# Products that nothing reads, ahead of and in the first part of an attention and two-layer kernel

## The chip, the cores and the metric

The kernel runs on one core of a Trainium2 chip. The metric is the device time of one execution in microseconds (us); less is better. A core has the matrix engine TensorE (PE; PEld is its loading of weights), VectorE (DVE), ScalarE (ACT), GpSimd (POOL) and SyncE (SP), which here only starts transfers (DMA). Each engine works through its own list of instructions in order and waits where an input is not there.

## The reference

Three stages follow one another. `_attn_ref` is a linear attention with decay, `_moe_ref` and `_moe2_ref` are products with weights:

```python
for t in range(S):                        # S = 768; B, H = 4, 8; D = 48
    state = alpha[:, :, t, :, None] * state + np.einsum('bhd,bhe->bhde', k[:, :, t], v[:, :, t])
    y[:, :, t] = np.einsum('bhd,bhde->bhe', q[:, :, t], state)
...
a = x @ w1                                # x: 3072 x 384, w1, w2: 384 x 1024
b = x @ w2
h = a * b @ w3                            # 1024 x 1024
return h @ w_out                          # 1024 x 384
...
h = x @ w_in                              # 384 x 2048
g = h * np.clip(h + 3.0, 0.0, 6.0) / 6.0
return g @ w_out                          # 2048 x 384
```

All inputs are float32 or, the weights, 64 bit floats.

## The kernel before, in words

**Attention** is cut into 24 units: six blocks of 512 tokens times four pairs of heads. A unit passes through steps `a0` to `a9` (`b5` to `b13` from unit 8 on). `a0` transposes the decay on PE into aT (four transposes, L301) and scans it on DVE (L313 to L324) into the running product P and its reverse r. `a1` transposes q (qT) and scales it (Q). `a2` uses the tile KT as scratch for a check on ACT (L341, L342) and transposes k (kT). `a3` multiplies kT by r into KT (DVE L347), so KT waits for L342. `a5` transposes KT back (kb, L385), and ACT copies that to Kn (L388). `score` makes the products sc of Q and KT (L358, plain fp32) and masks them into A; `a6` makes the state products u (L398) and the states T; `a8` the outputs py (L438, L446), which ACT copies to ys (L451). `a9` splits the result for the next stage.

**Weights** arrive as 64 bit words (`raw`, three buffers). A piece takes three ACT instructions (L72, L73, L76) and two on DVE (L81, L85) and then usually a split into a high and a low part (ACT L148, POOL L149). `w3` and `w_out` are folded into one matrix: `fold_t` transposes a piece of w3 (w3ps, L663) and splits it, `fold_mm` multiplies (facc; `mm3`, L152 to L154, three products for each pair). `l1_a` and `l1_b` are the products with w1 and w2 (w, the same lines), `l2` those with the folded matrix (acc, L723 to L726), `l3` and `l4` the second layer.

**Order.** A prologue runs over 33 gaps, `for g in range(npro)` at L872: each gap does the attention steps that are due (`attn_gap(g)`), some pieces of weight (`ws.step`) and, in a few gaps, a fold. A unit begins every sixth gap. The main loop (L883) then does an L1 step with three gaps each, so that attention runs on beside it. The written order is not the order of the engines: a scheduler goes through the program with a model of the times and puts each engine's instructions in an order of its own; only from step 46 of the main loop on is the written order kept (`MANUAL_FROM`). `ps_acc` has one PSUM buffer each of the tags acc0, acc1 and acc2; the folds use acc0 and acc1, the L2 sums all three. The tag asb in `tmp` has one buffer, which `l1_a` writes.

Of the kernel before, what the change touches and what calls it, by code (L numbers as in the profile page):

```python
# [8 lines left out]
F32 = mybir.dt.float32  # L9
# [9 lines left out]
P = 128  # L19
# [4 lines left out]
TB = 512  # L24
# [34 lines left out]
TBF = 1  # L59
ED = 16  # L60
SG = (5, 7, 9, 11, 14)
MANUAL_FROM = 46
RAWS = 3
RAW2 = 3
# [27 lines left out]
def attn_moe_kernel(  # L92
# [16 lines left out]
    nc = tc.nc  # L109
# [3 lines left out]
    def pool(stack, name, bufs, **kw):  # L113
        return stack.enter_context(tc.tile_pool(name=name, bufs=bufs, **kw))
# [6 lines left out]
    tmp = pool(main, "tmp", 2)  # L121
# [7 lines left out]
    ps_acc = pool(main, "ps_acc", 1, space=PSUM)  # L129
# [13 lines left out]
    over = const.tile([P, NB * NP], F32, tag="over", name="over")  # L143
    ones = const.tile([P, 2], F32, tag="ones", name="ones")
    nc.vector.memset(ones, 1.0)

    def split(hi, lo, x):
        nc.scalar.copy(out=hi, in_=x)  # L148
        nc.gpsimd.tensor_tensor(out=lo, in0=x, in1=hi.bitcast(F32), op=ALU.subtract)  # L149
# [462 lines left out]

    stages = {0: a0, 1: a1, 2: a2, 3: a3, SG[0]: a5, SG[1]: score, SG[2]: a6, SG[3]: a8, SG[4]: a9}
    stages2 = {0: a0, 1: a1, 2: a2, 3: a3, 5: b5, 6: b6, 9: b9, 12: b12, 13: b13, 15: a9}
# [3 lines left out]
    def begin(i):  # L618
        return 6 * i - min(max(i - U1, 0) // 2, 3)

    def attn_gap(g):
        for i in range(g // 6 - 2, g // 6 + 2):
            kk = g - begin(i)
            todo = stages if i < U1 else stages2 if begin(i) - begin(i - 1) == 6 else stages3
            if 0 <= i < len(units) and kk in todo:
                todo[kk](i)
# [32 lines left out]
    def fold_t(f, half):  # L659
        ps = ps_mm.tile([P, 4, P], F32, tag="mm", name="w3ps")  # L660
        w = w3n.pop((f, half))
        for g in range(4):
            nc.tensor.transpose(ps[:, g, :], w[:, g * P:(g + 1) * P], ident)  # L663
        hi = fs.tile([P, 4, P], F32R, tag="w3hi", name="w3hi")
        lo = fs.tile([P, 4, P], F32R, tag="w3lo", name="w3lo")
        nc.scalar.copy(out=hi, in_=ps)
        full = cv.tile([P, 4, P], F32, tag="u", name="w3full")
        nc.scalar.copy(out=full, in_=ps)
        nc.gpsimd.tensor_tensor(out=lo, in0=full, in1=hi.bitcast(F32), op=ALU.subtract)
        w3t[f, half] = (hi, lo)  # L670

    def fold_mm(f):
        if f < FOLDACC:
            acc = ps_acc.tile([P, DM], F32, tag=f"acc{f % KD}", name="facc")
        else:
            acc = ps_at.tile([P, DM], F32, tag="at", name="facc")
        for g in range(NM1):
            hi, lo = w3t[f, g // 4]
            mm3(acc, hi[:, g % 4, :], lo[:, g % 4, :], wo[g][0], wo[g][1], g == 0, g == NM1 - 1)
        hi = wts.tile([P, DM], F32R, tag=f"w34hi{f}", name="w34hi")  # L680
        lo = wts.tile([P, DM], F32R, tag=f"w34lo{f}", name="w34lo")
        nc.scalar.copy(out=hi, in_=acc)
        nc.vector.tensor_tensor(out=lo, in0=acc, in1=hi.bitcast(F32), op=ALU.subtract)
        w34[f] = (hi, lo)
# [110 lines left out]
    acc2 = {}  # L795
# [63 lines left out]
    for m in range(1, NM1 + 1):  # L859
        new = w3_items(m + AHEAD) + col_items(m)  # L860
        rest += new
        n = len(new)
# [5 lines left out]
    for what in INIT.split():  # L868
        n = int(what[1:])
        {"a": load_aqk, "v": load_v, "w": ws.issue}[what[0]](n)  # L870
    npro = 3 * LEAD
    for g in range(npro):  # L872
        attn_gap(g)
        ws.step(PC.get(g, 0))
        for f in PT.get(g, ()):
            fold_t(f, 0)
            fold_t(f, 1)
        if g in PF:
            fold_mm(PF[g])
# [3 lines left out]
    for si in range(n1 + 1):  # L883
        if si == MANUAL_FROM:
            manual.enter_context(tc.manual_schedule())
        g = npro + 3 * si
# [300 lines left out]
```

## Time and profile before

| | us |
|---|---|
| median of 3 runs | 910.4 (905.47 to 912.03) |
| profiled execution | 908.21 |
| its span, first to last instruction | 906.3 |
| PE busy | 870.2 (96%) |
| PEld, DVE, ACT, POOL busy | 735.0, 487.7, 380.6, 338.9 |

Times in the trace are us from the start of the span. A busy PE need not be one at its peak: matmuls are pipelined, so that in dense stretches the distance of two starts is shorter than the duration shown. A plain fp32 product gives two records in the trace, a transpose or a product of split (fp32r) operands one. "idle before <-X" is the engine's wait just before, and what ended it. The granted clock is the share of full speed (2.4 GHz) that TensorE was given; half is 1.2 GHz.

### The profile page before, as it was taken

What the parts mean: (1) busy time and instruction counts of PE and PEld (TensorE: products, weight loads), DVE (VectorE), ACT (ScalarE), POOL (GpSimd) and SP (SyncE); (2) the same over time, 40 slices, a digit from 0 to 9 for tenths busy, and PEclk for the clock granted to TensorE, in tenths of its full rate; (3) what the DMA queues carried; (4) which work ended last, traced back from release to release, by engine and by line L of the source; (5) the groups of instructions that cost most, each with busy time, mean ns of one, the idle gap of its engine ahead of it and who ended that gap; (6) DMA issues with size and microseconds to landing.
All of it is one profiled execution on the core that took longest, in us unless ns stands there. A gap on an engine that the chain in (4) does not pass through costs nothing.

```text
span 906.3 us, 16328 instructions
## 1 busy us (share of the span) xinstructions
PE 870.2 (96%) x6202; PEld 735.0 (81%) x6202; DVE 487.7 (54%) x844; ACT 380.6 (42%) x781; POOL 338.9 (37%) x310
## 2 busy tenths in 40 slices
PE   6889999999999999999899999999999999999995
PEld 5668888877787777777778898898898898888984
DVE  5987686767676778742646564333333333333331
ACT  5888888533343333434866663122121121121111
POOL 1544454412212222222755574342342342342331
PEclk9979999999999999999999999999999999999998
DMA  8785655453444544202543331001002002001001
GB/s 202 189 200 152 190 133 155 65 101 58 68 86 70 85 87 64 71 10 86 163 135 118 104 111 59 1 12 59 1 12 59 1 12 59 1 12 36 0 1 39
DMA packets 183431, 69.45 MB, mean 77 GB/s; under 512 B 154289, under 2 KB 172849, under 8 KB 183345
## 3 DMA queue, kind: packets, MB, share of 16 engines
q1 hardware_dynamic: 178992, 65.18, 30.5%
q10 hardware_dynamic: 4352, 3.15, 1.2%
q8 instruction: 51, 0.84, 0.4%
q14 instruction: 36, 0.29, 0.1%
HBM read 54.13 MB, written 9.44 MB: 70 GB/s over the span
## 4 chain that ended last, share of the span: by engine, by line
PE 80%; DMA 7%; ACT 5%; DVE 4%; SPq 2%; issue 2%; ACTq 0%; DVEq 0%
PE acc L808 7%; PE acc L811 7%; PE acc L809 7%; PE h L154 7%; PE h L153 7%; PE h L152 7%; PE w L152 6%; PE w L153 6%; PE w L154 6%; PE acc L726 3%; PE acc L723 3%; PE acc L724 3%; DMA raw<-in_moe_w_in 2%; DMA raw<-in_moe_w 2%; DMA out<-ot 1%
## 5 line engine op out<-in xcount | busy, mean ns | idle before, releaser
L149 POOL TENSOR_TENSOR glo<-g,ghi 128x512 fp32r<-128x512 f32 x96 | 126.0, 1313 | 236.8 <-ACT ghi L148 236.8
L785 DVE TENSOR_SCALAR t<-h 128x512 f32<-128x512 f32 x96 | 66.3, 691 | 236.3 <-PE h L154 236.3
L148 ACT CAST ghi<-g 128x512 fp32r<-128x512 f32 x96 | 59.7, 622 | 289.1 <-DVE g L787 267.3
L808 PE MATMUL acc<-wo2hi,ghi 128*128 128x384 f32 x384 | 130.7, 340 | 2.9 <-ACT ot L822 2.8
L809 PE MATMUL acc<-wo2lo,ghi 128*128 128x384 f32 x384 | 128.7, 335 | 0.0
L152 PE MATMUL w<-xhi,w 128*128 128x512 f32 x288 | 115.5, 402 | 7.3 <-ACT asb L703 7.3
L149 POOL TENSOR_TENSOR ablo<-ab,abhi 128x512 fp32r<-128x512 f32 x48 | 66.1, 1378 | 129.0 <-ACT abhi L148 121.9
L154 PE MATMUL h<-yhi,wilo 128*128 128x512 f32 x288 | 113.8, 395 | 0.0
L154 PE MATMUL w<-xhi,w 128*128 128x512 f32 x288 | 113.6, 394 | 0.0
L153 PE MATMUL h<-ylo,wihi 128*128 128x512 f32 x288 | 113.5, 394 | 0.0
L152 PE MATMUL h<-yhi,wihi 128*128 128x512 f32 x288 | 113.5, 394 | 0.0
L153 PE MATMUL w<-xlo,w 128*128 128x512 f32 x288 | 113.5, 394 | 0.0
L811 PE MATMUL acc<-wo2hi,glo 128*128 128x384 f32 x384 | 82.4, 335 | 0.0
L808 PEld LDWEIGHTS acc<-wo2hi,ghi 128*128 128x128 f32 x384 | 71.9, 187 | 9.6 <-ACT ot L822 4.4
L809 PEld LDWEIGHTS acc<-wo2lo,ghi 128*128 128x128 f32 x384 | 72.1, 188 | 4.3
L787 DVE SCALAR_TENSOR_TENSOR g<-t,h 128x512 f32<-128x512 f32 x96 | 66.0, 688 | 11.5 <-POOL glo L149 1.0
L152 PEld LDWEIGHTS w<-xhi,w 128*128 128x128 f32 x288 | 54.0, 188 | 20.8 <-ACT asb L703 9.7
L81 DVE SCALAR_TENSOR_TENSOR w<-u,w 128x384 uint32<-128x384 uint32 (+1 forms) x72 | 50.4, 702 | 37.4 <-ACT w L76 36.0
L811 PEld LDWEIGHTS acc<-wo2hi,glo 128*128 128x128 f32 x384 | 68.0, 188 | 0.0
L154 PEld LDWEIGHTS h<-yhi,wilo 128*128 128x128 f32 x288 | 53.9, 187 | 13.2
L154 PEld LDWEIGHTS w<-xhi,w 128*128 128x128 f32 x288 | 54.1, 188 | 11.7
L153 PEld LDWEIGHTS w<-xlo,w 128*128 128x128 f32 x288 | 54.1, 188 | 11.0 <-POOL xlo L149 0.4
(131 smaller groups left out, 1544.2 us busy)
## 6 DMA issues: line engine op xcount, KB each, us to landing
raw<-in_moe_w_out SPq DMA_DIRECT2D x24, 384.0 KB, 3.4
raw<-in_moe_w SPq DMA_DIRECT2D x16, 512.0 KB, 4.7
raw<-in_moe_w SPq DMA_DIRECT2D x16, 384.0 KB, 3.1
raw<-in_moe_w_in SPq DMA_DIRECT2D x16, 384.0 KB, 3.8
y<-yt SPq DMA_DIRECT2D x18, 256.0 KB, 2.3
yraw<-y SPq DMA_DIRECT2D x18, 256.0 KB, 2.9
vn<-in_v SPq DMA_DIRECT2D x32, 96.0 KB, 2.5
out<-ot SPq DMA_DIRECT2D x32, 96.0 KB, 2.2
```

Of the source, the lines that this page charges most:

```text
L81: nc.vector.scalar_tensor_tensor(out=low, in0=u.bitcast(U32), scalar=3, in1=low, op0=ALU.logical_shift_left, op1=ALU.bitwise_or,)
L148: nc.scalar.copy(out=hi, in_=x)
L149: nc.gpsimd.tensor_tensor(out=lo, in0=x, in1=hi.bitcast(F32), op=ALU.subtract)
L152: nc.tensor.matmul(out=dst, lhsT=lh, rhs=rh, start=start, stop=False)
L153: nc.tensor.matmul(out=dst, lhsT=lh, rhs=rl, start=False, stop=False)
L154: nc.tensor.matmul(out=dst, lhsT=ll, rhs=rh, start=False, stop=stop)
L723: nc.tensor.matmul(out=acc1[o], lhsT=wh[:, sl], rhs=hi, start=m == 0, stop=False)
L785: nc.vector.tensor_scalar(out=t, in0=ps, scalar1=3.0, scalar2=0.0, op0=ALU.add, op1=ALU.max)
L787: nc.vector.scalar_tensor_tensor(out=g, in0=t, scalar=6.0, in1=ps, op0=ALU.min, op1=ALU.mult)
L808: nc.tensor.matmul(out=acc2[o], lhsT=hi[:, sl], rhs=wh, start=m == 0, stop=False)
L809: nc.tensor.matmul(out=acc2[o], lhsT=hi[:, sl], rhs=wl, start=False, stop=False)
L811: nc.tensor.matmul(out=acc2[o], lhsT=lo[:, o * P:(o + 1) * P], rhs=wh, start=False, stop=m == NM2 - 1)
```

## The change

A tile `hot` of 128x512 is set to 0.5 by DVE, and `run_hot(n)` issues n products of its 128 first columns with its 256 first, in plain fp32, into the PSUM tile `heat`, which nobody reads. Five are written ahead of everything, and one behind the attention steps of each of the gaps 1 to 23: 28 in all. `heat` takes the tag acc2, `hot` the tag asb.

```diff
+HEAT = range(1, 24)
...
+    heat = ps_acc.tile([P, TB], F32, tag="acc2", name="heat")
+    hot = tmp.tile([P, TB], F32, tag="asb", name="hot", bufs=1)
+    nc.vector.memset(hot, 0.5)
+
+    def run_hot(n):
+        for _ in range(n):
+            nc.tensor.matmul(out=heat[:, :2 * P], lhsT=hot[:, :P], rhs=hot[:, :2 * P], start=True, stop=True)
+
+    run_hot(5)
...
     for g in range(npro):
         attn_gap(g)
+        if g in HEAT:
+            run_hot(1)
         ws.step(PC.get(g, 0))
```

The scheduler gives the engines another order with it. Lines of the changed kernel stand 11 further down (13 in the loops at the end), so its L312 is L301 of before.

PE at the start of the program, before:

```order
L301 MATMUL aT<-cs,al 112x128 x4
L301 MATMUL qT<-cs,qn 112x128 x4
L301 MATMUL kT<-cs,kn 112x128 x4
L385 MATMUL kb<-cs,KT 128x112 x4
L301 MATMUL aT<-cs,al 112x128 x4
L358 MATMUL sc<-Q,KT 128x128 x8
L663 MATMUL w3ps<-cs,w 128x128 x4
```

And PE there with the change:

```order
L154 MATMUL heat<-hot 128x256 x12
L312 MATMUL aT<-cs,al 112x128 x4
L312 MATMUL qT<-cs,qn 112x128 x4
L312 MATMUL kT<-cs,kn 112x128 x4
L154 MATMUL heat<-hot 128x256 x7
L674 MATMUL w3ps<-cs,w 128x128 x4
L154 MATMUL heat<-hot 128x256 x8
L396 MATMUL kb<-cs,KT 128x112 x4
L312 MATMUL aT<-cs,al 112x128 x4
L369 MATMUL sc<-Q,KT 128x128 x2
L674 MATMUL w3ps<-cs,w 128x128 x4
L369 MATMUL sc<-Q,KT 128x128 x2
```

The 28 products stand in four places, 12, 7, 8 and (behind the last row shown) 1, all of them ahead of unit 1's scores; the first w3ps has moved ahead of kb.

DVE at the start, before (edge is the scan's second operand, w a piece of weight):

```order
L145 MEMSET ones 128x2
L611 MEMSET edge 128x513
L313 TENSOR_SCALAR edge<-aT 112x4
L316 MEMSET aT 112x4
L317 SCALAR_TENSOR_TENSOR P<-aT,edge 112x512
```

And with the change:

```order
L146 MEMSET ones 128x2
L150 MEMSET hot 128x512
L622 MEMSET edge 128x513
L82 SCALAR_TENSOR_TENSOR w<-u,w 128x512
L86 SCALAR_TENSOR_TENSOR w<-raw,w 128x512
L324 TENSOR_SCALAR edge<-aT 112x4
L327 MEMSET aT 112x4
L328 SCALAR_TENSOR_TENSOR P<-aT,edge 112x512
```

The first piece of weight has moved from behind unit 0's KT to ahead of unit 0's first instruction.

ACT from the second piece of weight to L342 of unit 1, before, all of it:

```order
L72 ACTIVATE u<-raw 128x512
L73 ACTIVATE w<-raw,seven 128x512
L365 COPY A<-sc 128x512
L341 ACTIVATE KT<-al,amid 128x448
L76 ACTIVATE w<-w,seven 128x512
L666 CAST w3hi<-w3ps 128x512
L72 ACTIVATE u<-raw 128x384
L73 ACTIVATE w<-raw,seven 128x384
L342 ACTIVATE KT,over<-KT,adev 128x448
```

And the last twelve rows of the same stretch with the change, ahead of which stand thirteen more from the second piece on:

```order
L677 CAST w3hi<-w3ps 128x512
L679 COPY w3full<-w3ps 128x512
L334 COPY r<-edge 112x1
L73 ACTIVATE u<-raw 128x384
L74 ACTIVATE w<-raw,seven 128x384
L376 COPY A<-sc 128x512
L352 ACTIVATE KT<-al,amid 128x448
L159 CAST wohi<-w 128x384
L77 ACTIVATE w<-w,seven 128x384
L73 ACTIVATE u<-raw 128x384
L74 ACTIVATE w<-raw,seven 128x384
L353 ACTIVATE KT,over<-KT,adev 128x448
```

Where eight instructions stood ahead of L342 there are 24 now, most of them for pieces of weight that came later before.

## Rows read from the trace of the kernel before

**Rows 1.** The page, part 2: granted clock in 40 slices, in tenths.
```profile
PEclk9979999999999999999999999999999999999998
```

**Rows 2.** Busy time of each engine by stage; the first line names the columns.
```profile
core 0: us, PE busy (x) PEld busy (x) DVE busy (x) ACT busy (x) POOL busy (x), PEclk, DMA share, GB/s
0.00:20.00 20.00, 12.86 (x74) 10.62 (x76) 11.15 (x22) 9.52 (x18) 2.77 (x20) 1.00 0.87 204
...
47.00:68.00 21.00, 18.10 (x110) 14.70 (x111) 17.43 (x29) 17.43 (x38) 9.81 (x10) 0.68 0.80 202
68.00:280.00 212.00, 210.24 (x1900) 169.58 (x1900) 152.84 (x282) 123.94 (x266) 78.60 (x79) 1.00 0.51 110
```

**Rows 3.** Order of time, PE, 0 to 32: start, us, engine, line, operation, shapes, records.
```profile
4.45 1.07 PE L301 MATMUL aT<-cs,al 128*112 128x128 f32 x4 [4.45 <-DMA al<-in_alpha]
...
10.20 1.01 PE L385 MATMUL kb<-cs,KT 112*128 112x112 f32 x4 [2.64 <-DVE KT L347]
...
11.99 3.09 PE L358 MATMUL sc<-Q,KT 48*128 48x128 f32 x16
...
18.77 2.16 PE L438 MATMUL py<-A,vn 128*64 128x128 f32 x16
...
20.85 0.66 PE L663 MATMUL w3ps<-cs,w 128*128 128x128 f32 x4
...
23.40 0.62 PE L301 MATMUL aT<-cs,al 128*112 128x128 f32 x4 [0.90 <-ACT w3hi L666]
...
24.74 1.16 PE L358 MATMUL sc<-Q,KT 48*128 48x128 f32 x8
...
31.21 1.09 PE L438 MATMUL py<-A,vn 128*64 128x128 f32 x16
```

**Rows 4.** Order of time, PE, 64 to 85.
```profile
64.35 1.03 PE L446 MATMUL py<-Q,T 48*48 48x128 f32 x12 [0.52 <-DVE T L420]
...
68.34 0.34 PE L154 MATMUL facc<-wohi,w3lo 128*128 128x384 f32 x1
...
81.89 0.60 PE L301 MATMUL aT<-cs,al 128*112 128x128 f32 x4
...
84.18 0.33 PE L154 MATMUL facc<-wohi,w3lo 128*128 128x384 f32 x1
...
84.36 0.33 PE L152 MATMUL facc<-wohi,w3hi 128*128 128x384 f32 x1
```

**Rows 5.** Order of time, DVE, 0 to 22.
```profile
0.96 0.49 DVE L611 MEMSET edge<- 128x513 f32 x1
...
5.64 0.17 DVE L313 TENSOR_SCALAR edge<-aT 112x4 f32<-112x4 f32 x1 [4.20 <-PE aT L301]
...
9.46 0.69 DVE L347 TENSOR_TENSOR KT<-kT,r 112x512 f32<-112x512 f32 x1
...
12.21 0.69 DVE L85 SCALAR_TENSOR_TENSOR w<-raw,w 128x512 uint32<-128x512 uint32 x1
...
21.15 0.69 DVE L347 TENSOR_TENSOR KT<-kT,r 112x512 f32<-112x512 f32 x1 [0.70 <-ACT KT L342]
```

**Rows 6.** Order of time, ACT, second raw piece, L342 of units 1, 3, 5.
```profile
16.03 0.68 ACT L72 ACTIVATE u<-raw 128x512 f32<-128x512 f32 x1 [1.04 <-DMA raw<-in_moe_w]
...
20.38 0.66 ACT L342 ACTIVATE KT<-KT,adev 128x448 f32<-128x448 f32 x1
...
41.12 0.65 ACT L342 ACTIVATE KT<-KT,adev 128x448 f32<-128x448 f32 x1
...
75.71 0.67 ACT L342 ACTIVATE KT<-KT,adev 128x448 f32<-128x448 f32 x1
```

**Rows 7.** The chain that ended last: start, us, what.
```profile
72.19 1.09 PE sc L358 x8
...
98.11 0.23 PE w L152
```

## Prediction

> **What bounds the kernel now.** I read the clock line of the page first, then the busy times by stage, then PE, DVE and ACT in order of time, then the chain. The clock line [rows 1] is full nearly everywhere and dips in the third of its forty slices. By stage [rows 2], PE is busy 210.24 of 212 us from 68 to 280: from there on the time is PE's own list of work. Before 68 us PE waits for others: it has 12.86 busy us in the first 20, and 18.10 of 21 from 47 to 68 at a granted clock of 0.68. So only the first 80 us can change, and one mark tells by how much: the transposes of attention unit 6 (aT) start at 81.89 [rows 4]. In the order of before and of the change PE has the same products ahead of that mark (except the 28 new ones) and nearly the same order behind it, and DVE and ACT have converted 18 pieces of weight by then in both. If PE stays busy behind it, the time moves as that mark moves.
>
> The early low clock does not stand in the granted figure (1.00 for the first 20 us), but in durations [rows 3]: four transposes take 1.07 us at 4.45 and 0.62 at 23.40, the four of kb 1.01 at 10.20; the sixteen sc records 3.09 against 2 x 1.16; the sixteen py 2.16 against 1.09. The rise stands between the py at 18.77 and the w3ps at 20.85 (0.66). Eight groups of transposes at about 0.4 over, 0.77 for sc and 1.07 for py make 5.0 us of slow work. The dip from 47 to 68 costs 21 x (1 - 0.68) = 6.7 us of PE, in a stretch in which PE also had idle time. Together 11.7 us is all that a better clock could return.
>
> The Trainium skill (TensorE: Matmul & The Clock Gate, Part 1) puts the cost of warming up under 1% of a typical span, which would be 9 us here and speaks against a large gain. The early 5.0 us (0.6%) agrees, while with the later dip the rows come to 1.3%.
>
> **The change, part by part.** *The products.* Not five at the beginning and one per gap: in the order 12 stand ahead of everything, 7 behind the first twelve transposes (aT, qT, kT of unit 0), 8 ahead of kb and 1 in unit 0's scores. All 28 lie before unit 1's work, so nothing new runs near 47 us. A product of 128x256 in plain fp32 does not occur before. Bounds: from below, a py product of 128 columns, 1.09/8 = 0.14 us; from above, twice an sc product, 2 x 1.09/4 = 0.55 us [rows 3, 7]. I take 0.55, since sc is a plain fp32 product run one after another as these are. 28 x 0.55 = 15.4 us at full clock (3.9 by the lower bound). At the low clock sc shows up to twice this, so 1.1 us. The Trainium skill (FP8 and Floating Point Precision, TensorE Precision Notes) counts four passes for true fp32; with 0.23 us for a one-pass product of 512 columns [rows 7] that is an estimate of 0.46 each and 12.9 us in all.
>
> *When they end.* The memset of hot on DVE is as long as the one of edge, 0.49 us [rows 5], and ends near 1.5 us; PE starts there instead of at 4.45. How soon the clock rises has two rows: 10 us after work became dense at 10.20 [rows 3], and 4.0 us after 64.35, where records are back at 0.34 at 68.34 [rows 4]. In the quick case 4 us bring 3.6 products, and the other 8.4 take 4.6: the twelve end at 10.1. In the slow case 10 us bring 9.1 and the rest takes 1.6: 13.1. aT then follows 6 to 9 us later than before.
>
> *What hides that.* DVE's list has turned too: the first weight piece (L81, L85) now stands ahead of aT's scan. Its raw data and ACT's three steps are not sooner, so it ends where it did, at 12.21 + 0.69 = 12.90 [rows 5], and only then does the chain of unit 0 start, at 12.90 instead of 5.64: 7.3 us later when aT is there at 10.7, and 0.8 more in the slow case. The four and a half us from 5.64 to KT's end (9.46 + 0.69) follow: KT at 17.4. PE then still has qT, kT and w3ps (1.9 us) and 7 + 8 products (8.2): kb starts at 21 instead of 10.20, or at 23.5. ACT reads kb as its 13th instruction after 16.03, at about 22.5 by the pace below, which covers the quick case and leaves 1.6 us of the slow one open.
>
> *Unit 1.* Between the second raw piece at 16.03 and L342 of unit 1 ACT had 8 instructions in 4.35 us [rows 6], 0.54 each. Now 24 stand there: 24 x 0.54 = 13.1, so L342 at 29.1 and KT at about 30 instead of 21.15 [rows 5], 8.9 us late. In exchange five weight pieces are converted by then instead of two. DVE does not set this: it waited for ACT's L342 there before, too (the 0.70 idle at 21.15).
>
> *How the lag is paid back.* From unit 1's L342 to unit 5's ACT had 97 instructions (20.38 to 75.71) [rows 6], 0.57 each; up to unit 3's (41.12) 0.49. Now 88 remain. At 0.57 unit 5's comes at 29.1 + 50.2 = 79.3; at 0.49 at 72.2. I take the mean, 75.8, the same moment as before: weights done early are off ACT's list later. PE meanwhile has more to do between: ahead of unit 5's aT now stand 22 more products of the second fold, 6 of the first L1 and 4 more transposes; at 0.18 between starts [rows 4], 0.23 [rows 7] and 0.66 for the four [rows 3] that is 4.0 + 1.4 + 0.7 = 6.1 us of work moved ahead of unit 5. What before ran between unit 5's aT and the mark, part of it at the low clock, is then done in time that was idle. The mark follows KT of unit 5: L342 at 75.8, the product on DVE 1.5 us later, kb and aT: 78.5 instead of 81.89. With the two paces the mark is at 75 or 82; with the dip's pace (41.12 to 75.71, 55 instructions, 0.63) at 87.
>
> *Hidden at nothing:* heat's PSUM bank and hot's buffer are next used by the first L2 and L1 step, long behind the last of the 28. The memset of edge is 0.49 us later, and nothing reads edge before aT is there. DMAs: the first 26 on SP are the same; then three raw pieces stand ahead of unit 3's loads and each waits for DVE and ACT, so those loads leave a few us later, under a lag of 8.9 that hides them; without it they would be the next wait.
>
> **Sum.** 81.9 - 78.5 = 3.4 us gained. The profiled execution took 908.2 (span 906.3), which makes 904.8; against the median of 910.4, to which I refer the forecast, **907**. Its own range, from the paces 0.49 and 0.57, is 903 to 911.
>
> **Rivals.**
> Slower: the head is simply later. If ACT runs at the dip's 0.63, because PE's gaps from 18 to 30 us let the clock fall again and every chain of a unit gets longer, the mark comes at 87: +5, so 915. It decides once unit 5's L342 is later than 79. For it: the 8.9 us lag is certain and PE has gaps there. Against: facc products now stand between the attention products and fill them.
> Faster: ACT never waits after 29 us, because weights, which need no product, are always at hand. Where it works its instructions take 17.43/38 = 0.46 us each [rows 2]: unit 5's L342 at 69.6, the mark at 72.3, and 910.4 - 9.6 = 901. Against: from 20 to 41 us, with DMA and clock at their best, it needed 0.49.
> No effect: the new work fills only idle time, the lag is paid back exactly: 910, within 1 of it. For it: ACT's total list has not changed.
> [...]
>
> **Chances.** Likeliest 0.50, slower 0.22, faster 0.13, no effect 0.15. The range for 8 in 10 leaves out the outer part of both ends: 900 to 916. About 1% (9.1 us) is what a measurement can tell from no change here, the three runs of before spreading over 6.6 us. Faster by more than that (below 901.3) needs the faster rival nearly in full: 0.09. Slower (over 919.5) needs the slower one nearly twice over: 0.05. Within 1%: 0.86.
>
> **What would show it.** aT of unit 0 on PE between 10 and 14 us; DVE's first scan at 12.9; KT of unit 1 at 30; unit 5's L342 between 72 and 79; no slice of low clock from 47 to 68; the mark at 78.5, and everything behind it shifted by as much. It is wrong if the clock falls again between 18 and 60 us, if a product costs near 0.14 (then PE idles before kb), or if a wait behind the mark grows by more than the mark moved.

## The result, and the profile after

The changed kernel takes 917.94 us (median of 6 runs, 916.72 to 919.55) against 910.1 (6 runs of before beside it): 1.0096 times as long, interval 1.0074 to 1.0118 (the quotient of the two medians alone would be 1.0086). By the medians that is 7.8 us slower, 2 us beyond the upper end of the predicted range, and just inside the 1% that was called "within". The profiled execution took 917.69, its span 915.9.

By stage and by clock, the rows that answer to [rows 1, 2] (after; columns as there; lines of the changed kernel stand 11 further down):

```profile
PEclk9887999999999999999999999999999999999998
```

```profile
0.00:20.00 20.00, 18.18 (x87) 15.36 (x87) 7.91 (x16) 9.14 (x16) 1.42 (x18) 1.00 0.89 206
47.00:68.00 21.00, 17.50 (x125) 14.25 (x124) 16.20 (x25) 13.47 (x29) 9.73 (x9) 0.84 0.59 135
68.00:280.00 212.00, 210.26 (x1854) 169.64 (x1852) 154.28 (x284) 125.71 (x271) 76.98 (x79) 0.98 0.52 115
```

The dip from 47 to 68 has become shallower (0.84, before 0.68), but others have appeared ahead of it and behind it: the clock line is below 9 in three of its first four slices instead of one. In the stage 47 to 68 DVE and ACT are busy 1.2 and 4.0 us less than before, so they wait there although less of PE's time goes to the low clock.

PE at the start and at the mark, and DVE and ACT up to unit 5, in order of time (after):

```profile
1.49 7.83 PE L154 MATMUL heat<-hot 128*128 128x256 f32 x24 [1.49 <-DVE hot L150]
9.16 0.60 PE L312 MATMUL aT<-cs,al 128*112 128x128 f32 x4
...
10.47 3.19 PE L154 MATMUL heat<-hot 128*128 128x256 f32 x14
...
13.93 3.62 PE L154 MATMUL heat<-hot 128*128 128x256 f32 x16
17.39 0.55 PE L396 MATMUL kb<-cs,KT 112*128 112x112 f32 x4
...
73.56 0.66 PE L674 MATMUL w3ps<-cs,w 128*128 128x128 f32 x4 [1.74 <-DVE w L86]
...
87.94 0.60 PE L312 MATMUL aT<-cs,al 128*112 128x128 f32 x4
```

```profile
11.23 0.69 DVE L82 SCALAR_TENSOR_TENSOR w<-u,w 128x512 uint32<-128x512 uint32 x1 [9.24 <-ACT w L77]
...
12.56 0.16 DVE L324 TENSOR_SCALAR edge<-aT 112x4 f32<-112x4 f32 x1
...
16.37 0.69 DVE L358 TENSOR_TENSOR KT<-kT,r 112x512 f32<-112x512 f32 x1
...
28.76 0.68 DVE L358 TENSOR_TENSOR KT<-kT,r 112x512 f32<-112x512 f32 x1
```

```profile
27.69 0.66 ACT L353 ACTIVATE KT<-KT,adev 128x448 f32<-128x448 f32 x1
33.58 0.55 ACT L73 ACTIVATE u<-raw 128x384 f32<-128x384 f32 x1 [2.09 <-DMA raw<-in_moe_w_out]
...
49.11 0.67 ACT L73 ACTIVATE u<-raw 128x512 f32<-128x512 f32 x1 [2.92 <-DMA raw<-in_moe_w]
...
82.71 0.67 ACT L353 ACTIVATE KT<-KT,adev 128x448 f32<-128x448 f32 x1
```

The head is as foretold: the twelve products hold unit 0's transposes back to 9.16, DVE begins unit 0 at 12.56, its K product comes at 16.37, unit 1's at 28.76 [rows 5: 9.46 and 21.15]. ACT's check (L353, L342 of before) of unit 1 stands at 27.69. The lag is then not paid back: unit 5's check comes at 82.71 [rows 6: 75.71], the mark at 87.94 [rows 4: 81.89], 6.05 later. Behind the mark the span has 828.0 us against 824.4, another 3.5. Busy times of all that lies behind the mark, before and then after:

```profile
81.89:906.30 824.41, 803.87 (x5731) 682.98 (x5729) 425.18 (x732) 319.67 (x648) 305.51 (x264) 1.00 0.28 66
```

```profile
87.94:915.90 827.96, 807.37 (x5731) 686.25 (x5729) 425.99 (x731) 319.23 (x648) 307.11 (x263) 0.99 0.28 65
```

The same 5731 records, the same idle time of PE (20.54 and 20.59), and 3.5 us more busy time. Most of it is the clock: in both executions PE waits for ACT near 445 to 454 us, and in one of them the products behind the wait are slow, as they are behind another wait at 347.80. The nine steps from product to product behind each of the rows take 2.17 us at 444.58, but 3.69 at 347.80 and 3.54 at 453.94, which makes 2.9 of the 3.5 us. Order of time, before and then after:

```profile
444.58 0.50 PE L152 MATMUL w<-xhi,w 128*128 128x512 f32 x1 [2.65 <-ACT asb L703]
```

```profile
347.80 0.79 PE L163 MATMUL w<-xhi,w 128*128 128x512 f32 x1 [2.51 <-ACT asb L714]
...
453.94 0.80 PE L163 MATMUL w<-xhi,w 128*128 128x512 f32 x1 [2.56 <-ACT asb L714]
```

### The profile page after: what moved, and what is told of

It is laid out like the page before. It is cut to its first block, busy times and chain, and to the rows that moved or that the text cites. A ratio compares the mean times of both kernels' runs of the same rounds, so it can differ in the third digit from the quotient of the medians.

```text
span 915.9 us, 16431 instructions
## 1 busy us (share of the span) xinstructions
PE 884.9 (97%) x6258; PEld 748.5 (82%) x6258; DVE 487.3 (53%) x845; ACT 381.0 (42%) x781; POOL 339.4 (37%) x310
## 4 chain that ended last, share of the span: by engine, by line
PE 53%; DMA 4%; ACT 3%; DVE 1%; issue 1%; SPq 0%; ACTq 0%; DVEq 0%
PE acc L819 7%; PE acc L822 7%; PE acc L820 7%; PE h L165 7%; PE h L164 7%; PE h L163 7%; PE w L163 2%; PE w L164 2%; PE w L165 2%; DMA raw<-in_moe_w_in 2%; DMA out<-ot 1%; PE acc L734 1%; PE acc L735 1%; PE acc L737 1%; ACT ot L833 1%
## 5 line engine op out<-in xcount | busy, mean ns | idle before, releaser
L163 PE MATMUL w<-xhi,w 128*128 128x512 f32 x288 | 117.1, 408 | 7.0 <-ACT asb L714 7.0
L165 PE MATMUL w<-xhi,w 128*128 128x512 f32 x288 | 115.2, 400 | 0.0
L82 DVE SCALAR_TENSOR_TENSOR w<-u,w 128x384 uint32<-128x384 uint32 (+1 forms) x72 | 50.4, 702 | 42.9 <-ACT w L77 40.7
L163 PEld LDWEIGHTS w<-xhi,w 128*128 128x128 f32 x288 | 55.0, 191 | 20.4 <-ACT asb L714 8.7
L165 PEld LDWEIGHTS w<-xhi,w 128*128 128x128 f32 x288 | 55.0, 191 | 12.2 <-issue 0.2
```

The source lines that it names most:

```text
L82: nc.vector.scalar_tensor_tensor(out=low, in0=u.bitcast(U32), scalar=3, in1=low, op0=ALU.logical_shift_left, op1=ALU.bitwise_or,)
L163: nc.tensor.matmul(out=dst, lhsT=lh, rhs=rh, start=start, stop=False)
L165: nc.tensor.matmul(out=dst, lhsT=ll, rhs=rh, start=False, stop=stop)
```

## The experiments

The change does two things at once: it puts 28 products on PE, and it makes the scheduler bring all five engines' lists into another order. The second was taken apart from the first by editing the lists after the scheduler was done: a product that nobody waits for can be taken out of PE's list, or put in, without touching any other instruction. All lists but PE's (and DVE's, by the fill of the operand) are then those of the kernel named. One table for all; times are medians, each ratio is to runs of before made beside that kernel (medians 910.1 for the change, 910.92 for e1 to e4, 912.31 for e5 to e8, 911.19 for e9 to e12), so that the column of times is not to be compared across these groups. The other columns come from each kernel's own profile: unit 0's K product on DVE, ACT's check of units 1 and 5, the mark, and what lies behind it.

| kernel | order of | products | us | ratio to before (interval) | KT 0 | unit 1 | unit 5 | mark | behind |
|---|---|---|---|---|---|---|---|---|---|
| before | before | 0 | 910.4 | 1 | 9.46 | 20.38 | 75.71 | 81.89 | 824.4 |
| after | after | 28 early | 917.94 | 1.0096 (1.0074 to 1.0118) | 16.37 | 27.69 | 82.71 | 87.94 | 828.0 |
| e1_order_alone | after | 0 | 919.36 | 1.0084 (1.0065 to 1.0103) | 16.45 | 28.51 | 84.13 | 87.84 | 825.8 |
| e2_products_alone | before | 28 early | 914.78 | 1.0041 (1.0016 to 1.0066) | 14.27 | 25.07 | 82.98 | 89.16 | 825.0 |
| e3_five_alone | before | 5 at the front | 910.71 | 0.9988 (0.9975 to 1.0001) | 10.91 | 20.45 | 78.23 | 84.41 | 827.5 |
| e4_in_the_gaps | before | 28 in waits | 909.01 | 0.9973 (0.9957 to 0.9990) | 10.88 | 20.37 | 76.38 | 82.55 | 825.3 |
| e5_front_half | its own | 5 | 910.66 | 0.9987 (0.9963 to 1.0012) | 11.28 | 22.16 | 81.51 | 83.78 | 825.5 |
| e6_gap_half | its own | 23 early | 908.15 | 0.9974 (0.9948 to 1.0001) | 16.15 | 24.63 | 74.73 | 78.24 | 827.0 |
| e7_tiny | its own | 28 of one column | 914.16 | 1.0013 (0.9988 to 1.0039) | 14.90 | 25.88 | 80.94 | 87.26 | 824.9 |
| e8_again | after | 28 early | 918.64 | one run | 17.04 | 29.99 | 86.96 | 91.85 | 825.1 |
| e9_gap_order | e6 | 0 | 910.40 | 0.9992 (0.9969 to 1.0015) | 16.66 | 25.98 | 75.11 | 78.73 | 830.7 |
| e10_gap_order_28 | e6 | 28 early | 910.33 | 0.9990 (0.9968 to 1.0012) | 15.85 | 24.44 | 74.45 | 77.94 | 825.3 |
| e11_raw_earlier | after, one load moved | 28 early | 918.03 | 1.0075 (1.0049 to 1.0101) | 16.36 | 29.77 | 83.35 | 87.06 | 828.8 |
| e12_after_filled | after | 41 | 916.91 | 1.0052 (1.0028 to 1.0076) | 16.47 | 28.40 | 81.94 | 85.64 | 828.3 |

A profile is one execution: e8, the changed kernel once more, has its mark 3.9 later than the first and 2.9 less behind it, for a time 0.95 apart. So a mark is good to some 4 us, and a verdict below rests on the ratio and its interval, with the marks beside it.

**1. Order or products.** The first four kernels.

```diff
 e1:      attn_moe_kernel(tc, *args)          # behind the scheduler, in the changed kernel:
+    for i in [i for i in body if i.opcode == "Matmult" and i writes heat]:
+        body.remove(i)                       # 28
```

> The changed kernel, with its 28 products taken out of TensorE's list after the scheduler has placed everything; the lists of the five engines are otherwise those of the changed kernel, instruction by instruction. Theory A (the scheduler's new order costs the time: VectorE's first scan of unit 0 stands behind the w3 conversion that starts at 11.23, so unit 0 is late with or without products): the K product of unit 0 (16.37 with them, 9.46 before) still starts after 15, the transposes of unit 6's alpha start at 86 to 88.5, time 914 to 919. Theory B (the products' own time on TensorE and what is late behind it costs the time): that K product at 9.5 to 12, unit 6's transposes at 80 to 83.5, time 908 to 912.

Measured: 1.0084, K product of unit 0 at 16.45, mark at 87.84. The whole loss is there without one product:

```profile
16.45 0.69 DVE L358 TENSOR_TENSOR KT<-kT,r 112x512 f32<-112x512 f32 x1
```

```profile
87.84 0.60 PE L312 MATMUL aT<-cs,al 128*112 128x128 f32 x4
```

Theory B falls for the changed kernel. (The two rows are DVE's and PE's of e1.)

```diff
 e2:  (the kernel before, behind the scheduler; tile, count ahead of its first instruction)
+    [("aT" of unit 0, 12), ("kb" of unit 0, 15), (first "w3ps", 1)]
```

> The kernel before, its lists on every engine untouched, with the fill of the operand and the 28 products put into them after the scheduler: 12 ahead of unit 0's alpha transposes, 15 ahead of unit 0's kb, 1 ahead of the first w3ps, the places that they have in the changed kernel, as near as this order allows. It is the case that the prediction reckoned with. Theory A: unit 0's K product at 13.5 to 15, unit 0's kb at 17 to 18, but the 7 us are paid back over the next units: unit 6's alpha transposes at 78 to 84, time 906 to 912. Theory B: nothing is paid back, unit 6's transposes at 86 to 89, time 914 to 919. The prediction itself would have 78.5 and 907.

Measured: 1.0041 and 914.78. That is theory B's, at the lower end of its times, and not theory A's: the profiled execution has unit 0's kb at 17.52 and the mark at 89.16. PE's granted clock (the third figure from the end) was 0.70 from 30 to 47 us:

```profile
30.00:47.00 17.00, 16.77 (x113) 13.55 (x109) 13.00 (x27) 10.75 (x25) 7.44 (x7) 0.70 0.48 115
```

In the order of before the early products do cost, somewhat less than half of what the change cost, and the lag is not paid back here either. So each of the two, the new order without products (e1) and the products without the new order (e2), makes the kernel slower, and together they cost hardly more than the order alone. It is not quite the case that the prediction reckoned with, as the expectation has it: the prediction took the new lists of DVE and ACT, and this run has the old ones.

```diff
 e3:
+    [("aT" of unit 0, 5)]
```

> The kernel before, its lists untouched, with the fill and the five products of the very beginning alone, ahead of unit 0's alpha transposes. By the changed kernel's clock (up some 4.5 us after the first product) they end near 6, so the transposes start 1.5 us later than 4.45 and from there run in 0.60 us instead of 1.07. Theory A: time 908 to 912, no clear change. Theory B: half of what late products cost at most, 909 to 913. A theory C (the clock is what counts, and an early start of it pays) has 905 to 908 and a granted clock over 0.9 from 5 to 20 us.

Measured: 0.9988, no difference. The five run from 1.50 to 5.92. Of the transposes behind them the first group still takes 1.06 us and the third 0.60; then PE waits for DVE, kb is at 1.01 again, and the clock is at half from 10 to 20:

```profile
0.00:10.00 10.00, 6.45 (x22) 5.19 (x22) 3.75 (x10) 3.62 (x7) 1.26 (x17) 1.00 0.75 168
10.00:20.00 10.00, 8.34 (x52) 7.43 (x54) 7.87 (x14) 5.82 (x12) 1.59 (x3) 0.52 1.03 243
```

```profile
5.92 1.06 PE L301 MATMUL aT<-cs,al 128*112 128x128 f32 x4
...
7.34 0.60 PE L301 MATMUL kT<-cs,kn 128*112 128x128 f32 x4
11.66 1.01 PE L385 MATMUL kb<-cs,KT 112*128 112x112 f32 x4 [3.72 <-DVE KT L347]
```

The early start of the clock was lost at the next wait here; unit 1's check is at 20.45, as before. Theory C asked for a clock over 0.9 from 5 to 20 us, and that did not come about, so this run does not tell what such a clock would be worth. e9 and e10 below do, for another order.

```diff
 e4:
+    [("aT" 0, 5), ("kb" 0, 5), ("kb" 1, 1), ("aT" 2, 2), ("qT" 2, 1), ("kT" 3, 2), ("kb" 3, 1),
+     ("aT" 4, 1), ("py" 2 from T, 3), ("kb" 4, 1), ("aT" 5, 4), ("py" 3 from T, 2)]
```

> The kernel before, its lists untouched, with the fill and 28 products in places where TensorE waited in the trace of before: 5 at the front, 5 ahead of unit 0's kb (idle 2.64 there), and 18 between 21 and 65 us ahead of the transposes, kb and state products that waited 0.3 to 1.9 us. It is the change as its wording has it, where the scheduler can't move the products forward. Theory C (a clock kept up is what pays): granted clock over 0.95 from 47 to 58 us, where it was near 0.5, unit 6's alpha transposes at 76 to 80 instead of 81.89, time 903 to 908. Theories A and B say that the clock of the prologue is not what sets the end there: the dip goes or not, unit 6's transposes at 81 to 84, time 909 to 912.

Measured: 0.9973, 0.3% faster. From 47 to 58 the clock is full, where before it was 0.54 in the same stage (before, then e4):

```profile
47.00:58.00 11.00, 10.85 (x49) 8.66 (x50) 7.75 (x12) 8.80 (x19) 4.58 (x6) 0.54 0.88 225
```

```profile
47.00:58.00 11.00, 9.57 (x84) 6.88 (x82) 7.11 (x13) 8.13 (x17) 4.47 (x5) 1.00 0.79 203
```

and yet the mark is at 82.55, not earlier than 81.89. The low clock of that stretch was worth 11 x 0.46 = 5.1 us of PE's time; by the ratio 2.5 us came back in all (0.9 to 3.9 by the interval), so at least a part of it was cover under waits for DVE and ACT. The small gain is real by its interval and touches the upper end of theory C's times, but where it lies these profiles don't show.

**2. The halves of the change, and the change without its length.**

```diff
 e5: -HEAT = range(1, 24)          e6: -    run_hot(5)          e7: -  heat[:, :2 * P] ... rhs=hot[:, :2 * P]
     +HEAT = range(0)                  +    run_hot(0)              +  heat[:, :1] ... rhs=hot[:, :1]
```

> One half of the change in the source: the five products at the very beginning, none in the gaps, and the scheduler plans with them. It does not give the order of before back: on VectorE one weight conversion now stands ahead of unit 0's K product (none before, one in the changed kernel), 3 ahead of unit 1's (2 and 5), 6 ahead of unit 2's (4 and 9). Theory A (weights pulled ahead of the attention units make the head late, and the lateness reaches the mark, unit 6's alpha transposes, whole or nearly): the K product of unit 2 is 1.5 to 4 us later than 30.61, the mark at 83 to 86, time 911 to 914. A theory that only the products' own TensorE time counts has 910 to 911, as the five alone in the order of before gave no difference.

> The other half in the source: the 23 products of the gaps, none at the very beginning, planned by the scheduler. It puts twelve of them ahead of unit 0's alpha transposes and the rest before unit 1's, as in the changed kernel, and on VectorE 1, 4, 7, 11, 13 and 16 weight conversions ahead of the K products of units 0 to 5 (before: 0, 2, 4, 8, 12, 16; the changed kernel: 1, 5, 9, 12, 14, 17). Theory A: nearly all of the loss, the mark at 85 to 88, time 914 to 918. If instead the two halves had a share each by the number of products, this half would be at 916 to 917 and the front half at 911 to 912.

> The changed kernel with products of one column instead of 256, so that they take TensorE next to no time, for the scheduler too. It still reorders: on VectorE 1, 4, 7, 11, 13 and 18 weight conversions ahead of the K products of units 0 to 5. Theory A (the new order is the cost, and it comes from the presence of 28 more instructions, not from their length): the K product of unit 1 later than 24, the mark at 84 to 88, time 912 to 918. Theory B (the products' TensorE time): as before, 909 to 912.

Measured: 0.9987, 0.9974 and 1.0013. e5 has unit 2's K product at 37.89, later still than expected, a mark at 83.78, and no loss. e7 has theory A's mark (87.26), but no loss that its interval can tell from nothing: 914.16 is in A's range, but before took 912.31 beside it, and so the verdict is open. e6 refutes theory A: nearly as many products early, DVE's weight conversion ahead of unit 0, unit 0's K product at 16.15 as late as in the changed kernel, and the mark 9.7 earlier, ahead even of before's. Order of time, PE and DVE, in e6:

```profile
1.49 7.22 PE L154 MATMUL heat<-hot 128*128 128x256 f32 x24 [1.49 <-DVE hot L150]
8.55 0.60 PE L312 MATMUL aT<-cs,al 128*112 128x128 f32 x4
...
78.24 0.60 PE L312 MATMUL aT<-cs,al 128*112 128x128 f32 x4
```

```profile
16.15 0.69 DVE L358 TENSOR_TENSOR KT<-kT,r 112x512 f32<-112x512 f32 x1
```

So a late head can be paid back, and here the mark comes where the prediction had it (78.5). The two halves do not add up to the whole: each comes with an order of its own and is harmless, and together they cost 1%.

> The changed kernel once more, for a second profile of it. The time is split at the start of unit 6's alpha transposes (the mark). If the new order costs before the mark alone, the mark stands again at 87.5 to 88.5 and what lies behind it is 824 to 828, the 4 us of spread coming from the clock, which fell after a wait of 2.2 us or more on TensorE near 345 and 450 us in the first profile and cost some 1.7 us each time; with no fall behind the mark it would be 824 to 825. If the order also costs behind the mark, that part is 827 or more whether or not the clock falls there.

Measured (one profile, 918.64): the mark at 91.85, outside what was expected, and 825.1 behind it, with one fall of the clock there (0.83 from 450 to 460). So the changed kernel's part behind the mark can be nearly as short as before's (824.4), and most of the first profile's 3.5 us came from falls of the clock, which come and go between executions. Not all of the spread is that: e11 and e12, in nearly the same order, have 828.8 and 828.3 with one fall each.

**3. The order, or what PE does in it.** Busy times between unit 1's check and unit 5's check, in the kernel before, in the changed kernel and then in e6 (columns as in [rows 2]):

```profile
20.38:75.71 55.33, 46.88 (x346) 36.72 (x343) 46.50 (x82) 45.71 (x103) 27.74 (x25) 0.88 0.74 184
```

```profile
27.69:82.71 55.02, 47.48 (x352) 37.71 (x352) 43.17 (x78) 40.71 (x93) 22.51 (x22) 0.83 0.68 166
```

```profile
24.63:74.73 50.10, 43.66 (x385) 33.44 (x386) 41.55 (x81) 40.92 (x93) 26.07 (x24) 0.98 0.77 180
```

The changed kernel has 5.0 us less work on ACT here than the kernel before, and is hardly faster through it (55.02 against 55.33): ACT waits 14.3 us instead of 9.6. e6 has the same 93 records on ACT and 40.9 us of work, takes 50.10 and waits 9.2. With the 3.1 us by which unit 1's check is later, and 1.7 from unit 5's check to the mark (5.23 against 3.51), that is the 9.7. Two causes are open here: the order, or the clock (0.83 against 0.98).

```diff
 e9:  (e6, behind the scheduler)          e10: (e6, behind the scheduler)
+    body.remove(i)   # all 23            +    5 more products behind the first
```

> The gap half (908.15, mark 78.24), with its 23 products taken out of TensorE's list after the scheduler has placed everything; the other lists are the gap half's. The gap half's head is as late as the changed kernel's (K product of unit 0 at 16.15 against 16.37), and yet it is faster than the kernel before, so theory A in its first form (a late head is lost for good) has fallen. Theory A2 (what decides is the whole order that the scheduler came to, not the products): mark 77 to 81, time 906 to 911 without them too. Theory C2 (this order is good only because the products hold the clock at full from 30 to 68 us): the clock falls somewhere between 20 and 68, mark 82 to 87, time 911 to 916.

> The gap half's order once more, with five more products put in after the scheduler, right behind the first, so that all 28 run, 17 of them ahead of unit 0's transposes. Theory A2: five more products of 0.45 us are 2.3 us more in a head that waits for VectorE until 12.6 anyway, so the mark is at 78 to 82 and the time 908 to 912, though the number of products is that of the changed kernel (918). Theory B2 (the products' time counts after all, beyond some number): 915 or more.

Measured: 0.9992 and 0.9990, marks at 78.73 and 77.94, as theory A2 had it. e6's order costs nothing with 0, 23 or 28 products on PE (0.9992, 0.9974, 0.9990), the changed kernel's order costs 0.8 to 1.0% with 0 or 28 (1.0084, 1.0096). In e9 no product runs, the clock is at 0.57 and 0.58 from 10 to 30 us, in e10 at 1.00 and 0.66, and the mark does not mind (e9, then e10):

```profile
10.00:20.00 10.00, 3.70 (x15) 2.96 (x16) 6.86 (x12) 5.14 (x10) 0.15 (x1) 0.57 1.00 237
20.00:30.00 10.00, 10.00 (x66) 8.09 (x66) 8.17 (x19) 9.37 (x22) 6.33 (x6) 0.58 0.76 170
```

```profile
10.00:20.00 10.00, 9.70 (x62) 8.38 (x60) 7.16 (x13) 5.34 (x11) 0.15 (x1) 1.00 1.04 245
20.00:30.00 10.00, 8.78 (x62) 6.71 (x64) 8.51 (x18) 8.97 (x22) 7.99 (x6) 0.66 0.82 199
```

B2 falls for this order; in the order of before the products do cost (e2). C2 falls as it was put: without products the clock still is 0.96 from 30 to 47 and 0.95 from 47 to 68, so the products are not what holds it there. What a low clock from 30 to 68 would cost in this order was not tried.

```diff
 e11: (the changed kernel, behind the scheduler, SP's list)
-    qn, kn, kn, kn, kn, raw          # raw: the twelfth weight load, 512 KB
+    raw, qn, kn, kn, kn, kn
```

> The changed kernel with one weight load of 512 KB moved ahead of five small loads (one of q, four of k, unit 3) on SP's list, after the scheduler. In the changed kernel this load was issued at 44.99 and ScalarE waited 2.92 us for it until 49.11, with unit 3's check (53.43) and K product (54.90) behind it. Theory A2 in its detail (ScalarE stands waiting for weight loads, 2.09 us at 33.58 and 2.92 at 49.11, because the new order asks for them earlier while SP issues them no earlier): the second wait falls to 0 to 1.2, unit 3's K product and the mark come 1.5 to 3 earlier in median, time 914.5 to 916.5. If that wait is only where some other lateness shows, the wait moves to another instruction and the time stays at 917 to 919.

Measured: 1.0075, mark at 87.06. The wait was cut from 2.92 to 1.31, and three us later ACT waited 1.34 for something else:

```profile
49.67 0.69 ACT L73 ACTIVATE u<-raw 128x512 f32<-128x512 f32 x1 [1.31 <-DMA raw<-in_moe_w]
...
52.81 0.62 ACT L159 CAST xhi<-xflat 128x512 fp32r<-128x512 f32 x1 [1.34 <-DMA xflat<-ys]
```

The wait moved, as the second branch had it, and the ratio shows no gain clear of noise. The edit did less than it was to do: the load was issued at 45.61, not ahead of the 44.99 of the changed kernel, and SP stood idle for 1.6 us just ahead of it. Counted from unit 1's check it left 1.5 us earlier. So this run takes that one wait out in part; it does not clear the waits for loads as a group.

```diff
 e12: (the changed kernel, behind the scheduler)
+    3 products ahead of the fourth wohi product, 4 ahead of unit 2's u, 2 ahead of the fourth w3ps, 4 ahead of the fifth
```

> The changed kernel with 13 more products, put in after the scheduler at four places where TensorE waited 0.8 to 1.9 us: 3 ahead of the fourth wohi product (35.11), 4 ahead of unit 2's state products (52.12), 2 ahead of the fourth w3ps (55.03), 4 ahead of the fifth (73.56). Theory C2 (in the changed kernel the clock falls in the waits, to 0.71 at 35 to 40, 0.50 at 55 to 60 and 0.5 at 75 to 85 us, and TensorE at half pace is what keeps the lateness from being paid back): clock over 0.9 in 47 to 80, mark at 82 to 86, time 911 to 915. Theory A2 (the order decides, TensorE's pace is hidden): mark 87 to 90, time 917 to 920.

Measured: 1.0052, mark at 85.64. The clock stood at 1.00 all the way between the two checks:

```profile
28.40:81.94 53.54, 48.61 (x416) 38.38 (x415) 43.28 (x82) 40.71 (x93) 21.73 (x21) 1.00 0.71 171
```

The same 93 records and 40.71 us of work take 53.54 instead of 55.02, where e6's order takes 50.10. The time lies between both theories (C2 had 911 to 915, A2 917 to 920). With the clock at full there the loss is still clear of noise, so the low clock is not needed for it. What share the clock has these runs do not measure: the ratio overlaps with those of e1 (1.0084) and e11 (1.0075), e11 has the same 53.58 us between the checks at a clock of 0.87, and the 13 added products may themselves cost something. What does hold across all profiles is the split by order: the stretch takes 53.54 to 56.97 us in the five profiles of the changed kernel's order (after, e1, e8, e11, e12) and 49.13 to 50.10 in the three of e6's (e6, e9, e10), with products or without.

What ACT waits for there, summed over its rows, is raw loads of weight for 5.7 to 10.0 us in the five and 3.4 to 4.8 in the three, and PE for 1.2 to 5.6 against 0.5 to 1.5. In e12 the waits for PE fell to 1.2 us (5.1 in the changed kernel) and those for loads rose to 10.0 (6.6), most of it in two places:

```profile
49.96 0.67 ACT L73 ACTIVATE u<-raw 128x512 f32<-128x512 f32 x1 [3.57 <-DMA raw<-in_moe_w]
...
80.57 0.55 ACT L73 ACTIVATE u<-raw 128x384 f32<-128x384 f32 x1 [3.35 <-DMA raw<-in_moe_w]
```

No version beat the kernel before by more than e4 and e6 (0.3%, and e6's interval reaches 1.0001).

**What stays open.** Which of the order's many differences costs the 5 us between the checks wasn't isolated. The lists differ in how much weight stands ahead of each unit: ahead of the K products of units 1 to 5 DVE has 5, 9, 12, 14 and 17 conversions in the changed kernel, 4, 7, 11, 13 and 16 in e6, 2, 4, 8, 12 and 16 before, and 21 ahead of unit 6's in each. One conversion is 1.4 us of DVE and about 2 us of ACT (three instructions, the first 0.67). Counted from the start, ACT has 16 instructions ahead of unit 1's check before, 24 in e6 and 30 in the changed kernel; the last six, at the 0.54 us that the prediction read, make 3.2 us, about the 3.1 by which that check is later. But e5 and e7 also have weights ahead and no loss that their intervals show. That the waits for raw loads cost the rest is likely and not shown. An exchange of single instructions between two orders wasn't tried, since the waits of all engines count on their places.

## Why the prediction was wrong, point by point

- **A product's price.** Predicted 0.55, measured 3.62/8 = 0.45 at full clock. The bounds held, the choice of the nearer row was 20% too high. The Trainium skill (FP8 and Floating Point Precision, TensorE Precision Notes), by whose four passes the estimate was 0.46, is borne out by that row.
- **The head.** Right. aT followed the twelve products at 9.16 (foretold 10.1 for their end), DVE began unit 0 at 12.56 (12.90), unit 0's K product ended at 17.06 (17.4), unit 1's check came at 27.69 (29.1), its K product at 28.76 (30). The size of the first price put aT and kb too late in the forecast, kb most (17.39, foretold 21); the other marks hang on DVE's and ACT's lists.
- **The pay-back. This step failed.** "I take the mean, 75.8" put unit 5's check between two of ACT's paces, 0.49 and 0.57 us per instruction. It came at 82.71: 88 instructions in 55.0 us, 0.63, the dip's pace, which was the slower rival's, with the mark at 87 (measured 87.94). The fault was to take a pace for a property of ACT. ACT's work fell as the counts said (40.7 us for 93 records, 45.7 for 103 before), but its waiting rose by nearly as much (14.3 us, 9.6 before), and how long it waits goes with the order, which no pace of the old order tells. e6 shows how near the step was to coming true (unit 5's check at 74.73, mark 78.24). A count of ACT's list tells the two apart up to unit 1's check (24 instructions from the start against 30), but not behind it: both have 93 records between the checks, and take 50.10 and 55.02 us.
- **"Weights done early are off ACT's list later"** is right as a count (21 conversions ahead of unit 6's K product in every order) and wrong as a time: ACT waited for raw loads of weight (2.09 at 33.58, 2.92 at 49.11) that the new order asks for earlier.
- **The slower rival** had the size (915; measured 917.94) and the mark, but its cause only in part: "because PE's gaps let the clock fall again". The clock did fall (0.83 between the checks), and with it held at 1.00 (e12) about half of the loss remained, and the mark came 2.3 earlier, which is within what two profiles of one kernel differ by; with no product at all (e1, clock 0.88 there) the loss was whole. So its number came near the result while its cause is not shown.
- **No low clock from 47 to 68** was wrong (0.84). It came true in e6's order, whose products run early as well (1.00 in e6 and in e10). The dip's 6.7 us stood in the prediction as a ceiling, and as that it held: e4 removed the dip from 47 to 58, the mark stayed, and 0.3% came back.
- **Everything behind the mark shifts alike** held for the work (5731 records, the same idle time) and not for the clock, which fell after waits that ended at 347.80 and 453.94 in this execution.
- **The sum.** 6.05 at the mark and 3.5 behind it against the profiled 906.3 make the span of 915.9; against the median of 910.4, to which the forecast was referred, it is 7.5.
- **The early 5.0 us of low clock.** e3 does not tell what they are worth, since its clock was at 0.52 again from 10 to 20. In e6's order they were worth nothing that can be measured: e9 (0.57 from 10 to 20) has 0.9992 and e10 (1.00) 0.9990. The Trainium skill (TensorE: Matmul & The Clock Gate, Part 1) puts the cost of warming up under 1% of a typical span, and these two runs agree.

## What to carry to other kernels

Where a scheduler sets the order, an instruction that nobody reads is still an edit of every engine's list: look at what the new order does to the units at the head, and measure the order apart from the instruction, by taking the instruction out again behind the scheduler. A pace read from the old order does not tell whether a lag is paid back; count the work and the waits apart, for only the work follows from the list, and give the two outcomes equal chances when the rows cannot tell them apart. A low clock on an engine that waits for others can be cover and not cost (e9 against e10); test it before counting it as gain.

## What the runs showed of the hardware

- The granted clock falls after some waits of PE and not after others of the same length: a wait of 2.65 at 444.58 was followed by a product of 0.50 us, one of 2.56 at 453.94 by one of 0.80. It need not fall at once: in e8 the product behind a wait of 2.63 at 455.07 takes 0.50, and the slow ones (0.63) begin 1.3 us later. Behind the mark the profiles show none to three such places (near 280, 345 and 450 us) and 824.4 to 830.7 us in all. The number of falls does not by itself order these times: e7 has two and 824.9, e11 one and 828.8.
- The first twelve products of the changed kernel fit two paces: five at 0.93 (e3's five take 4.64 us) and seven at 0.456 (3.19 us, as the seven behind 10.47) make the 7.83 us of the row at 1.49. By this the clock rose behind the fifth or so, which is an estimate, as the row is not split.
- Early products did not hold it when PE then waited: from 10 to 20 us it was at 0.52 behind five (e3, wait of 3.72) and 0.68 behind ten (e4, wait of 1.65). In e10, where PE hardly waited there, it was at 1.00.
